# RWKV-6 attention into a tanh-shrink MLP: the first block prepared half by half, and raw weights loaded as pairs of w_in or of w_out tiles

## The chip, the cores and the metric

The kernel runs on one core of a Trainium2 chip. The metric is device time of one execution in microseconds (us). The core has four computing engines that work side by side, each through its own queue in order: PE (TensorE, matrix products into PSUM), DVE (VectorE), ACT (ScalarE) and POOL (GpSimd). SP (SyncE) does no arithmetic here; it issues DMA transfers, in order as well. Data lie in SBUF (128 partitions), results of PE in PSUM (8 banks of 512 float32 a partition).

## What is computed

```python
# attention: batch 4, heads 8, sequence 768, head size 48
for t in range(S):
    cur = einsum('bhd,bhe->bhde', u * k[t], v[t])
    y[:, :, t] = einsum('bhd,bhde->bhe', r[t], state + cur)
    state = w[t][..., None] * state + einsum('bhd,bhe->bhde', k[t], v[t])
# MLP on the 3072 tokens, model size 384, hidden size 2048
x = y.transpose(0, 2, 1, 3).reshape(B * S, H * D)
h = x @ w_in
out = (h - tanh(h)) @ w_out
```

w, the decay, lies between 0.8 and 0.95. Everything is float32.

## The kernel before, in words

**Tiling.** The 3072 tokens are cut into eight blocks of 384 (`Block(b, q)`: four batch rows, two halves of the sequence). A block's attention is done in six chunks of 64 tokens, for four pairs of heads; heads go in *halves* of two pairs each, first pairs 2 and 3, then 0 and 1 (`HALVES = (UP, 0)`). The block's MLP runs over 16 tiles (f) of 128 hidden units. While a block's MLP runs, the attention of the next block is prepared in between, from a plan written by hand (`plan(i)`), so that PE never lacks work. The first block has nobody to prepare it: a function `boot` does so before the MLP starts.

**Attention of a half.** `behind` (L403) scans w backwards inside each chunk: the product of all decays behind a token. `take_whole` (L423) picks out each chunk's whole decay. `before` (L391, L392) scans forwards. `times_behind` (L417) multiplies k by the first scan, `times_before` (L410) r by the second, and `times_u` (L428, ACT) scales k by u in place. `turn` (L487, L489) transposes the decayed k on PE and copies it out as `ks`. `own` and `earlier` are small products on PE (L463) that give the scores of a token with itself and with earlier tokens of its chunk; a predicated copy on DVE with a mask (L470) puts each into `scores`. `update_1` (L537) forms k times v for each chunk on PE, and `update_2` (L549) carries the states from chunk to chunk on DVE. `from_states` (L603) and `from_scores` (L620) add both parts of the result up in PSUM. `result_out` (L654) copies it into `xT`, and `fill_holes` (L661) moves the fourth pair, `late`, into the free rows of the three xT tiles by six small DMAs. `bound` (L434) and `held` (L439) gather what a check at the end needs.

**MLP of a tile.** `first` (L767) multiplies w_in by xT into PSUM (`hp`), ACT copies it out as h (L770), DVE squares it (L796), ACT forms qa (L799), DVE does two products (L773), and PE multiplies by w_out into three accumulators (`acc`, L844), which in block 0 follows three tiles behind `first`. Later blocks form 15 products of sums in place of 18 (`Fewer`, L891).

**Weights.** They come as 64-bit numbers in 16 units of 768 KB; unit f holds w_in and w_out of tile f (`load_weights`, L246). `convert` turns one unit into float32 by three ACT instructions (L260) and one DVE instruction (L264). Five raw buffers exist; a load into one waits until the buffer's last unit is converted. `more_weights` issues the next load on SP, and `begin_behind` makes a load wait for a named instruction.

**Order.** PE, SP, DVE and ACT run in the order in which the code issues (`manual_schedule`). In `boot`, SP issues w, k and r of the first half, the same of the second half, v and three raw units; further raw units follow behind conversions. PE starts with 97 tiny products of the identity (`passed`, L293) and later fills waits with wide ones whose result nobody reads (`busy`, L285). The second half's `behind` to `earlier` follow the first's, then one `update_1` and one `update_2` for all four pairs, `from_states` for all pairs, and `from_scores` half by half. Three units and one piece of a fourth are converted by the time tile 0 starts; then one unit a tile. `boot` has a PSUM pool of its own with four tiles of two banks, closed before the main part's pools open (one bank for hp, three for acc, two tiles of two banks for the attention). DVE clears the whole of `scores` and parts of both `states` at the start.

Of the kernel before, what the change touches and what calls it, by code (L numbers as in the profile page):

```python
# [74 lines left out]
LAST = 5  # L75
LATE = 3
# [46 lines left out]
def kernel(  # L123
# [50 lines left out]
    nc.gpsimd.memset(mask_all[0:L], 1.0)  # L174
# [5 lines left out]
    for m, at in mask_cols.items():  # L180
        if isinstance(m, str):
            masks[m] = mask_all[:, at]
            half = masks[m][0:L]
            keep(half, -1 if m == "above" else 0, [[1, L]], -1)
            if m == "diagonal":
                keep(half, 0, [[-1, L]], 1)
                continue
        else:
            width, step = (2, 1) if m == 1 else (m, 0)
            nb = L // (2 * m)  # L190
            masks[m] = mask_all[:, at].rearrange("s (b j) -> s b j", j=width)
            half = masks[m][0:L]
            keep(half, 0, [[-2 * m, nb], [0, width]], 1)
            keep(half, m - 1, [[2 * m, nb], [step, width]], -1)
        if m == "above":
            nc.gpsimd.tensor_copy(out=mask_all[L:P, 0:128], in_=mask_all[0:L, 0:128])
    nc.gpsimd.tensor_copy(out=mask_all[L:P, 128:], in_=mask_all[0:L, 128:])

    A = const.tile([P, 2, NPAIR, NCP, L], F32, name="scores", tag="scores")
    nc.vector.memset(A, 0.0)  # L200

    states = []
    for q in range(NQ):
        st = const.tile([P, NPAIR, NCH, L], F32, name=f"states{q}", tag=f"states{q}")
        nc.vector.memset(st[:, :, :, D:], 0.0)
        states.append(st)
    nc.vector.memset(states[0][:, :, 0, :], 0.0)

    w_sb = const.tile([P, NF, 2 * DM], F32, name="w_sb", tag="w_sb")
    w_in_sb = w_sb[:, :, 0:DM].rearrange("p f (i c) -> p f i c", i=KC)  # L210
    w_out_sb = w_sb[:, :, DM:2 * DM]
# [30 lines left out]
    nc.vector.memset(ones, 1.0)  # L242

    def load_weights(f, queue):
        raw = conv.tile([P, 2 * DM, 2], I32, name="raw", tag="raw")
        ins = queue.dma_start(out=raw, in_=weights[f].bitcast(I32).rearrange("p (n two) -> p n two", two=2))  # L246
        return f, raw, ins

    def convert(f, raw, _):
# [4 lines left out]
        a = w_sb[:, f, :].bitcast(I32)  # L254
# [22 lines left out]

    def scratch(ps):
        return ps.tile([P, 2, BANK], F32, name="att", tag="att")

    def busy(to, n):

        by = ident.bitcast(BF16)
# [3 lines left out]

    def passed(to, n):


        by = ident.bitcast(BF16)[:, 0:16]
        for _ in range(n):
            nc.tensor.matmul(to[0:16, 0:16], lhsT=by, rhs=by, start=True, stop=True, skip_group_check=True)  # L293
# [3 lines left out]
    class Block:  # L297
# [97 lines left out]
        def behind(self, p0, n):  # L395
            a, width = p0 * NCH * LP, n * NCH * LP
            t = self.half("post", p0, width + 1)
            nc.gpsimd.memset(t[:, width:], 1.0)
# [49 lines left out]
        def gram(self, ps, lhs, rhs, p0, n, m=None):  # L448
            width = L // 2 if m else L
            ps_t = scratch(ps)  # L450
            used = ps_t[:, :, 0:n * NCP * width]
            gr = used.rearrange("s h (p c t) -> s h p c t", p=n, c=NCP)
            for p in range(p0, p0 + n):
                for c in range(NCP):
                    for h in range(2):
                        for par in range(2):
# [6 lines left out]
                            nc.tensor.matmul(dst, lhsT=self.chunk(lhs, p, 2 * c + par)[rows], rhs=src,  # L463
                                             start=True, stop=True)
            return used

        def masked(self, ps, lhs, rhs, mask, p0):
            gr = self.gram(ps, lhs, rhs, p0, UP)
            mask = mask.bitcast(U8).unsqueeze(1).unsqueeze(1)
            return lambda: nc.vector.copy_predicated(  # L470
# [4 lines left out]
        def own(self, ps, p0):  # L475
            return self.masked(ps, "k", "r", masks["diagonal"], p0)
# [533 lines left out]
    def boot(ps, blk, later):  # L1010
        h1, h2 = HALVES
        for p0 in HALVES:
            for name in ("w", "k", "r"):
                blk.load(name, p0, UP)
# [290 lines left out]
```

## Time and profile before

| what | value |
|---|---|
| median of three runs | 558.15 us (556.01 to 560.48) |
| the profiled execution's own time | 556.46 us |
| its span, first to last instruction | 554.7 us |
| mean granted clock of PE | 0.997 |
| HBM read, written | 44.73 MB, 4.72 MB |
| shares of the chain that ended last | PE 94%, ACT 2%, DVE 2% |
| tile 0's first product starts at | 29.47 us |

The span is shorter than the execution by 1.76 us, which lie around it. In rows of the timeline the columns are start and duration in us, engine, line, operation, written tile, read tiles, shape and count; in brackets stands how long the engine had nothing to do before, and what ended that. A row of a fp32 product counts two passes, so 48 in a row are 24 products in the code. The ends of PE's rows are modelled. The main part's PE rows are almost without holes from 38.6 us on, so most of what can be seen of a change to the boot lies in the first 40 us.

### The profile page before, as it was taken

How to read it: one execution, taken by the hardware profiler on the slowest of the kernel's cores; microseconds unless marked ns; L12 is line 12 of the kernel's file. 1: busy time of each engine (PE TensorE's matmuls, PEld its weight loads, DVE VectorE, ACT ScalarE, POOL GpSimd, SP SyncE). 2: the span in 40 equal slices, each digit the busy share in tenths (PEclk: the TensorE clock that was granted, in tenths of full speed). 3: DMA queues.
4: the chain of work that ended last, by engine and by line, in shares of the span. 5: the costliest groups of instructions: out<-in, count | busy, mean ns of one | idle time of the engine just before them, and what ended most of it. 6: DMA issues, size and time to landing. Idle time of an engine off the chain costs nothing.

```text
span 554.7 us, 14151 instructions
## 1 busy us (share of the span) xinstructions
PE 537.9 (97%) x5726; PEld 404.7 (73%) x5726; DVE 463.3 (84%) x947; ACT 402.2 (73%) x811; POOL 12.0 (2%) x40
## 2 busy tenths in 40 slices
PE   4899999999999999999999999999999999999996
PEld 4646566578787787777778787777877777787774
DVE  8789999989989989878997989969897897557563
ACT  3889896697766886688866886688865986666561
POOL 6100000000000000000000000000000000000000
PEclk9999999999999999999999999999999999999999
DMA  8598473244302432236311531136122320100101
GB/s 304 207 320 301 165 215 107 72 122 115 116 13 85 100 118 74 62 94 134 109 54 44 144 116 62 52 89 157 58 88 67 80 65 4 54 1 0 44 2 46
DMA packets 53030, 56.31 MB, mean 102 GB/s; under 512 B 21472, under 2 KB 50912, under 8 KB 52960
## 3 DMA queue, kind: packets, MB, share of 16 engines
q1 hardware_dynamic: 52576, 55.18, 33.6%
q8 instruction: 46, 0.75, 0.5%
q14 instruction: 24, 0.20, 0.1%
q10 hardware_dynamic: 288, 0.10, 0.1%
q0 software_dynamic: 96, 0.07, 0.1%
HBM read 44.73 MB, written 4.72 MB: 89 GB/s over the span
## 4 chain that ended last, share of the span: by engine, by line
PE 94%; ACT 2%; DVE 2%; issue 1%; DMA 1%; SPq 0%; DVEq 0%; ACTq 0%
PE hp L767 44%; PE acc L891 26%; PE att L891 6%; PE acc L844 6%; PE att L463 2%; PE att L603 2%; PE att L620 2%; PE acc L869 2%; PE att L537 2%; DMA r<-in_rT 1%; ACT up L260 1%; PE att L487 1%; DVE scores L470 0%; PE att L285 0%; DVE pre L392 0%
## 5 line engine op out<-in xcount | busy, mean ns | idle before, releaser
L767 PE MATMUL hp<-xT,w_sb 128*128 128x384 f32 x768 | 270.1, 488 | 1.3 <-ACT h L770 1.1
L767 PEld LDWEIGHTS hp<-xT,w_sb 128*128 128x128 f32 x768 | 137.3, 190 | 75.9 <-ACT h L770 3.3
L770 ACT ACTIVATE h<-hp 128x384 f32<-128x384 f32 x128 | 62.7, 490 | 104.8 <-PE hp L767 104.7
L891 PE MATMUL acc<-forms,g 128*128 128x128 f32 x954 | 133.7, 276 | 0.5
L891 PEld LDWEIGHTS acc<-forms,g 128*128 128x128 f32 x954 | 121.6, 192 | 10.3 <-issue 1.3
L773 DVE SCALAR_TENSOR_TENSOR h<-h,s 128x384 f32<-128x384 f32 x128 | 70.7, 552 | 53.9 <-ACT s L788 53.8
L814 DVE TENSOR_TENSOR g<-g 128x256 f32<-128x256 f32 x265 | 103.3, 419 | 7.8 <-PE acc L891 7.0
L789 ACT ACTIVATE qa<-s,shift 128x384 f32<-128x384 f32 x113 | 69.6, 616 | 3.7
L791 ACT ACTIVATE junk<-s,shift 128x384 bf16<-128x384 f32 x113 | 67.7, 600 | 0.0
L773 DVE SCALAR_TENSOR_TENSOR g<-qa,h 128x384 f32<-128x384 f32 x112 | 61.7, 551 | 1.8 <-ACT qa L799 0.2
L788 ACT ACTIVATE s<-h 128x384 f32<-128x384 f32 x113 | 59.1, 523 | 3.6
L891 PEld LDWEIGHTS acc<-w_sb,g 128*128 128x128 f32 x318 | 46.7, 191 | 9.7 <-ACT sums L859 0.3
L891 PE MATMUL acc<-w_sb,g 128*128 128x128 f32 x318 | 53.1, 276 | 0.1
L891 PE MATMUL att<-w_sb,g 128*128 128x128 f32 x212 | 35.5, 275 | 0.0
L891 PEld LDWEIGHTS att<-w_sb,g 128*128 128x128 f32 x212 | 31.1, 192 | 5.3
L926 DVE TENSOR_TENSOR sums<-sums 128x256 f32<-128x256 f32 x84 | 32.9, 408 | 1.6 <-ACT sums L903 1.3
L844 PE MATMUL acc<-w_sb,sums 128*128 128x384 f32 x96 | 33.9, 489 | 0.1
L260 ACT ACTIVATE up<-raw 128x768 f16<-128x768 f32 (+1 forms) x32 | 32.0, 1070 | 0.0
L392 DVE TENSOR_TENSOR_SCAN pre<-w,start 128x780 f32<-128x780 f32 x16 | 28.5, 1783 | 0.5
L403 DVE TENSOR_TENSOR_SCAN post<-w,seed 128x780 f32<-128x780 f32 x16 | 28.5, 1783 | 0.2 <-DMA w<-in_wT 0.2
L844 PEld LDWEIGHTS acc<-w_sb,sums 128*128 128x128 f32 x96 | 17.9, 190 | 12.0 <-issue 0.2
L791 ACT ACTIVATION_READ_ACCUMULATOR junk<-s,shift 128x1 f32 x113 | 21.1, 187 | 0.0
(93 smaller groups left out, 506.5 us busy)
## 6 DMA issues: line engine op xcount, KB each, us to landing
raw<-in_weights SPq DMA_DIRECT2D x16, 768.0 KB, 5.8
w<-in_wT SPq DMA_DIRECT2D x7, 780.0 KB, 4.6
k<-in_kT SPq DMA_DIRECT2D x7, 768.0 KB, 4.5
r<-in_rT SPq DMA_DIRECT2D x7, 768.0 KB, 4.5
v_sb<-in_v SPq DMA_DIRECT2D x8, 576.0 KB, 3.9
k<-in_tokens SPq DMA_DIRECT2D x7, 576.0 KB, 3.9
r<-in_tokens SPq DMA_DIRECT2D x7, 576.0 KB, 4.9
out_y<-sums SPq DMA_DIRECT2D x18, 128.0 KB, 1.8
```

The costliest lines, as they stand in the source:

```text
L260: return lambda: nc.scalar.activation(out=to, in_=of, func=AF.Copy, scale=scale, bias=bias)
L392: return nc.vector.tensor_tensor_scan(out=self.tile("pre")[:, cols], data0=self.tile("w")[:, cols], data1=start[:, 0:n * NCH * LP], initia ...
L767: nc.tensor.matmul(hp, lhsT=w_in_sb[:, f, kc, :], rhs=xT[kc], start=(kc == KC - 1), stop=(kc == 0))
L770: return h, nc.scalar.activation(out=h, in_=hp, func=AF.Copy, scale=1.0 / UPSCALE)
L773: return lambda: nc.vector.scalar_tensor_tensor(out=out, in0=in0, scalar=scalar, in1=in1, op0=op0, op1=ALU.mult)
L788: nc.scalar.activation(out=s, in_=h, func=AF.Square)
L789: nc.scalar.activation(out=qa, in_=s, func=AF.Square, bias=shift[:, 4:5])
L791: nc.scalar.activation(out=junk[:, 0:NB], in_=s, func=AF.Relu, bias=shift[:, 5:6], accum_out=excess[:, at:at + 1])
L814: return lambda: nc.vector.tensor_tensor(out=G[:, to:to + 2], in0=two(G, g_at(q, a0), g_at(q, a1)), in1=two(G, g_at(q, b0), g_at(q, b1)), ...
L844: nc.tensor.matmul(acc, lhsT=g[:, j * P:(j + 1) * P], rhs=w_out_sb[:, f, :], start=(f == self.first), stop=(f == NF - 1))
L891: nc.tensor.matmul(to, lhsT=G[:, g_at(q, a), :], rhs=rhs, start=start, stop=stop, skip_group_check=True)
L926: ops.append(lambda op=op, at=at: nc.vector.tensor_tensor(out=at[0], in0=at[1], in1=at[2], op=OPS[op]))
```

## The change

**Loads.** Block 0's w is loaded into the tile that later holds states 0 (`states0`) and not into the tile `w`, so block 1's w has no old contents to wait for. SP issues: w of pair 3, w of pair 2, k and r of the first half, w of the second half, one raw unit, k of the second half, v, r of the second half. Three raw units, block 1's w and k and so on follow in the order of the code below, each behind the instruction named in `begin_behind`.

**Raw units.** A unit now holds w_in of two tiles or w_out of two tiles (`UNITS`), still 768 KB. The order is w_in of tiles 0 and 1, w_in of 2 and 3, w_out of 0 and 1, w_in of 4 and 5, w_out of 2 and 3, and so on. `boot` converts three units. After that `converting` issues ACT's part in pieces, a third of a unit each, by the list `PIECES` (2, 1, 2, then 3 a tile up to tile 9, then 4 a tile up to tile 12, and one piece more inside tile 1); the DVE instruction follows a tile later, ahead of the tile's other DVE work.

**Boot by halves.** The first half is taken to its end, states and result included, before the second half's result. `update_half` forms k times v for one half with the chunks side by side, `totals_by_column` (ACT) writes the chunk decays in the same layout, and `states_half` carries the states by one scan of 288 columns a pair and one small add. `from_states` reads these `first_states`. The first half's result has all its parts done before `result_out` of pairs 3 and 2; the second half's predicated copy is cut in two, so that pair 1 and pair 0 can follow one another.

**PSUM.** The main part's pools are opened before the boot, with the four banks of hp and acc as one tile. The boot takes turns among two pairs of these banks and the two attention tiles. Tiles 0, 1 and 2 write hp into three different banks.

**Memsets.** `scores` is cleared by ACT from `start`; the memsets of `states` are gone or moved (POOL, tile 14); `ones` goes to POOL; four of the masks are drawn only in the branch that is not taken here.

**Fillers.** The 97 tiny products go, as do the wide fillers before tiles 1, 2 and 3. The first `own` has 8 wide fillers ahead and 7 more that read a copy of the identity which ACT makes behind the first half's totals (`later_ident`); 2 stand ahead of the second `earlier` and 4 ahead of its `from_states`. `bound` of block 0 moves from the boot to tiles 13 and 14.

```diff
+PIECES = 2, 1, 2, 3, 3, 3, 3, 3, 3, 3, 4, 4, 4
+UNITS = [(0, 0), (0, 1)] + [u for j in range(NF // 2 - 2) for u in ((1, j), (0, j + 2))] + [(1, NF // 2 - 2),
+                                                                                      (1, NF // 2 - 1)]
...
-    nc.vector.memset(A, 0.0)
+    nc.scalar.copy(out=A.rearrange("s h p c t -> s (h p c t)").rearrange("s (n t) -> s n t", t=BANK),
+                   in_=start[:, 0:BANK].unsqueeze(1).to_broadcast([P, 2 * NPAIR * NCP * L // BANK, BANK]))
...
+        def update_half(self, ps, p0):
+            self.by_column = scratch(ps)[:, :, 0:D * NCH].rearrange("d p (e c) -> d p e c", c=NCH)
+            for x in range(UP):
+                if x:
+                    nc.tensor.drain().then_inc(fence, 1)
+                    fences.append(None)
+                    nc.tensor.wait_ge(fence, len(fences))
...
+        def totals_by_column(self, p0):
+            of = self.whole(p0, UP).rearrange("d (p c) -> d p c", c=NCH)[:, :, 1:]
+            nc.scalar.copy(out=first_totals[:, p0:p0 + UP, :, 1:],
+                           in_=of.unsqueeze(2).to_broadcast([P, UP, D, NCH - 1]))
+
+        def states_half(self, p0):
+            for p in range(UP):
+                to, by, kv = (t.rearrange("d e c -> d (e c)") for t in
+                              (first_states[:, p0 + p], first_totals[:, p0 + p], self.by_column[:, p]))
+                nc.vector.tensor_tensor_scan(out=to, data0=kv, data1=by, initial=0.0, op0=ALU.add, op1=ALU.mult)
+            return lambda kv=self.by_column: nc.vector.tensor_tensor(
+                out=states[1][:, p0:p0 + UP, 0, 0:D], in0=first_states[:, p0:p0 + UP, :, NCH - 1],
+                in1=kv[:, :, :, 0], op=ALU.add)
...
     def boot(ps, blk, later):
         h1, h2 = HALVES
+        blk.tiles["w"] = states0
+        for name, p0, n in (("w", h1 + 1, 1), ("w", h1, 1), ("k", h1, UP), ("r", h1, UP), ("w", h2, UP)):
+            blk.load(name, p0, n)
+        more_weights(nc.sync)
+        blk.load("k", h2, UP)
         blk.load_v()
+        blk.load("r", h2, UP)
...
+        blk.behind(h1 + 1, 1)
+        blk.behind(h1, 1)
         blk.take_whole(h1, UP)
+        blk.totals_by_column(h1)
+        nc.scalar.copy(out=later_ident, in_=ident)
         blk.before(h1, UP)
         blk.times_behind(h1, UP)
         blk.times_u(h1, UP)
-        blk.turn(ps, h1, ahead=97)
-        own = blk.own(ps, h1)
+        own = blk.own(ps, h1, ahead=8, late=7)
+        blk.turn_1(ps, h1)
         blk.times_before(h1, UP)
         earlier = blk.earlier(ps, h1)
-        blk.bound(h1)
-        blk.bound(h2)
+        begin_behind(blk.done, more_weights(nc.sync))
         blk.behind(h2, UP)
         blk.take_whole(h2, UP)
+        first_a, first_b = convert(*raws.pop(0))
+        run(first_a[:1])
+        blk.turn_2(h1)
+        run(first_a[1:2])
+        blk.update_half(ps, h1)
         own()
         blk.times_behind(h2, UP)
         blk.times_u(h2, UP)
-        blk.turn(ps, h2)
-        own = blk.own(ps, h2)
+        blk.turn_1(ps, h2)
+        blk.turn_2(h2)
         earlier()
+        run(first_a[2:])
+        blk.totals_by_column(h2)
+        blk.results(ps, halved=True)
+        blk.result("from_scores", both[0])
+        blk.states_half(h1)()
+        blk.result("from_states", both[0], True)
+        begin_behind(blk.opened, more_weights(nc.sync))
         blk.before(h2, UP)
+        own = blk.own(ps, h2)
+        blk.update_half(ps, h2)
         blk.times_before(h2, UP)
-        blk.update_1(ps)
...
+        earlier = blk.earlier(ps, h2, ahead=2)
+        blk.result_out((3,), nc.scalar.copy)
+        blk.result_out((2,))
+        blk.fill_holes([nc.sync, nc.gpsimd])
+        begin_behind(blk.done, later.load("w"))
+        more_weights(nc.sync)
         second_a, second_b = convert(*raws.pop(0))
         third_a, third_b = convert(*raws.pop(0))
+        run(second_a)
+        own()
+        onwards = blk.states_half(h2)
+        blk.results(ps, halved=True)
+        busy(blk.yp[0][:, 0], 4)
+        blk.result("from_states", both[1])
+        earlier(1, 1)
+        earlier(0, 1)
+        begin_behind(third_a[0](), more_weights(nc.sync))
+        run(third_a[1:2])
+        later.load("k")
         more_weights(nc.sync)
...
+        for p in reversed(both[1]):
+            blk.result("from_scores", (p,), True, more=True)
+        onwards()
         run(first_b)
         blk.result_out((1,), nc.scalar.copy)
         blk.result_out((0,), nc.vector.tensor_copy)
         run(third_a[2:])
         run(second_b)
         run(third_b)
         blk.held(0, NPAIR)
...
-            if i == 0 and f in (1, 2, 3):
-                busy(acc[0], 2)
-            h, made = first(here, f, ps_d)
+            h, made = first(here, f, banks[:, 0 if i else {1: 1, 2: 2}.get(f, 0), 0:NB])
...
+            extra = converting(pieces, PIECES[f] if f < len(PIECES) else 0) if not i else []
...
+            if i == 0 and f in (NF - 3, NF - 2):
+                blk.bound(HALVES[f - NF + 3])
+            if i == 0 and f == NF - 2:
+                nc.gpsimd.memset(states[0][:, :, 0, 0:D], 0.0)
```

More of the change, by code (lines that the diff above doesn't have):

```diff
@@ L1051, in boot @@
-        more_weights(nc.sync)
-        own()
-        blk.results(ps)
-        blk.result("from_scores", both[0])
-        run(blk.update_2())
-        run(second_a)
-        blk.result("from_states", ALL, cs=(0, 1), more=True)
-        earlier = blk.earlier(ps, h2)
-        run(third_a[:2])
-        blk.result("from_states", ALL, cs=(2,))
-        earlier()
-        idle = scratch(ps)[:, 0]
-        busy(idle, 2)
-        blk.result_out((3,), nc.scalar.copy)
-        blk.fill_holes([nc.sync, nc.gpsimd])
@@ L1116 @@
             xT = later.begin()
[L1117 removed]
+        phases, before, ahead, loads, formed_w = plan(i)
         row0 = blk.b * S + blk.q * NB
```

252 lines of the change are left out of this document (132 added, 120 removed).

## The prediction

> **What bounds the kernel now.** I read first the page's part 1 and the span, then the table of windows, then the chain of work that ended last, then each engine's timeline over the first 50 us, then the DMA issues one by one.
>
> ```profile
> span 554.7 us, 14151 instructions
> PE 537.9 (97%) x5726; PEld 404.7 (73%) x5726; DVE 463.3 (84%) x947; ACT 402.2 (73%) x811; POOL 12.0 (2%) x40
> ```
> ```profile
> 22.00:23.50 1.50, 0.22 (x14) 0.08 (x6) 0.95 (x3) 1.50 (x3) 0.00 (x0) 1.00 1.01 410
> 25.50:28.00 2.50, 2.35 (x50) 1.64 (x51) 0.82 (x2) 2.41 (x4) 1.38 (x3) 0.50 0.21 57
> 29.50:38.60 9.10, 7.88 (x25) 3.74 (x25) 6.88 (x13) 6.87 (x11) 0.00 (x0) 1.00 1.03 399
> 38.60:60.00 21.40, 21.40 (x150) 13.43 (x151) 20.58 (x37) 20.67 (x30) 0.00 (x0) 1.00 0.79 260
> 60.00:100.00 40.00, 39.90 (x396) 24.32 (x395) 38.00 (x69) 30.73 (x52) 0.13 (x2) 1.00 0.51 158
> ```
> The window rows read: stretch, length, then busy time of PE, PEld, DVE, ACT, POOL, the granted clock, DMA share, GB/s. From 38.6 on PE is busy 21.40 of 21.40 us, then 39.90 of 40.00. So the span is the moment at which PE becomes saturated plus a fixed rest, and whatever the boot saves arrives at the end one for one, as long as no later wait takes it. The change works almost wholly before that moment. I therefore price one thing: how much earlier PE reaches tile 4's first product, which started at 42.54.
>
> ```profile
> 29.47 2.17 PE L767 MATMUL hp<-xT,w_sb 128*128 128x384 f32 x6
> 42.54 2.10 PE L767 MATMUL hp<-xT,w_sb 128*128 128x384 f32 x6
> ```
> What holds the boot is VectorE. Its timeline (start, duration):
>
> ```profile
> 4.31 1.78 DVE L403 TENSOR_TENSOR_SCAN post<-w,seed 128x780 f32<-128x780 f32 x1 [0.17 <-DMA w<-in_wT]
> 6.67 1.78 DVE L392 TENSOR_TENSOR_SCAN pre<-w,start 128x780 f32<-128x780 f32 x1
> 8.37 0.93 DVE L417 TENSOR_TENSOR post<-k,post 128x768 f32<-128x768 f32 x1
> 9.22 0.96 DVE L410 TENSOR_TENSOR pre<-r,pre 128x768 f32<-128x768 f32 x1
> 10.11 1.89 DVE L403 TENSOR_TENSOR_SCAN post<-w,seed 128x780 f32<-128x780 f32 x1
> 12.53 1.03 DVE L470 COPY_PREDICATED scores<-mask_all,att 128x768 f32<-128x768 uint8 x1 [0.33 <-PE att L463]
> 13.45 0.94 DVE L417 TENSOR_TENSOR post<-k,post 128x768 f32<-128x768 f32 x1
> 19.08 0.36 DVE L549 TENSOR_TENSOR states<-att,whole 128x192 f32<-128x192 f32 x1
> 22.66 0.35 DVE L549 TENSOR_TENSOR states<-states,att 128x192 f32<-128x192 f32 x1
> 24.05 1.01 DVE L470 COPY_PREDICATED scores<-mask_all,att 128x768 f32<-128x768 uint8 x1 [1.03 <-PE att L463]
> 24.96 0.94 DVE L264 SCALAR_TENSOR_TENSOR w_sb<-w_sb,up 128x768 int32<-128x768 int32 x1
> 27.57 1.12 DVE L654 COPY xT<-att 48x384 f32<-48x384 f32 x2 [1.68 <-ACT up L260]
> ```
> It starts when the first w has landed and runs nearly without a hole to 23.0; ten state updates stand from 19.08 to 23.0 (first and last shown), then come two waits, 1.03 for scores and 1.68 for ScalarE. ScalarE is the second chain:
>
> ```profile
> 19.38 0.90 ACT L260 ACTIVATE w_sb<-raw 128x768 f32<-128x768 f32 x1
> 20.18 2.00 ACT L260 ACTIVATE up<-raw 128x768 f16<-128x768 f32 x2
> 22.01 0.90 ACT L260 ACTIVATE w_sb<-raw 128x768 f32<-128x768 f32 x1
> 24.52 0.97 ACT L654 COPY late<-att 48x384 f32<-48x384 f32 x2 [0.66 <-PE att L603]
> 31.73 0.49 ACT L770 ACTIVATE h<-hp 128x384 f32<-128x384 f32 x1 [2.24 <-PE hp L767]
> 33.95 0.59 ACT L799 ACTIVATE qa<-s,shift 128x384 f32<-128x384 f32 x1
> 89.11 0.48 ACT L654 COPY late<-att 128x384 f32<-128x384 f32 x1 [2.37 <-PE att L620]
> ```
> One raw unit costs it 22.01 - 19.38 = 2.63.
>
> **The change, step by step.** I use start-to-start steps of the rows (they are a little shorter than durations), and take the edits in the order of the path.
>
> *Start.* The first w comes as two loads of one pair each. SP issued w, k, r of the first half, the same of the second, and v 0.51 apart from 0.93 to 4.00, then the first raw unit 0.7 later; the second fence gives KB and us from issue to landing of one issue each (the r is the second half's; the last raw is the one issued at 28.1 behind block 1's w).
>
> ```profile
> 0.93 0.47 SPq L346 DMA_DIRECT2D w<-in_wT  x1
> 4.00 0.67 SPq L381 DMA_DIRECT2D v_sb<-in_v  x1
> ```
> ```profile
> w<-in_wT SPq DMA_DIRECT2D x1, 390.0 KB, 3.4
> u_sb<-in_uT ACTq DMA_DIRECT2D x1, 2.0 KB, 2.3
> r<-in_rT SPq DMA_DIRECT2D x1, 384.0 KB, 7.8
> v_sb<-in_v SPq DMA_DIRECT2D x1, 576.0 KB, 8.9
> raw<-in_weights SPq DMA_DIRECT2D x1, 768.0 KB, 10.1
> raw<-in_weights SPq DMA_DIRECT2D x1, 768.0 KB, 5.9
> ```
> 390 KB landed at 4.3, 2316 KB in all at 11.3, 2892 at 12.9, 3660 at 14.8. A load of 195 KB lies between the smallest load (0.93 + 2.3 = 3.2) and 4.3: I take 3.75, nearer the middle because the bytes halve. Two scans of 390 columns then end near 5.5 instead of 6.1. The memsets taken off VectorE are free in themselves (it waited 0.17 for w), but they would stand in the way at 3.75. Their replacement on ScalarE (1536 zeros, two small copies) fills time in which it had nothing to do until k's product at 8.4. The first mask copy of scores needs those zeros only at 11.6. POOL's shorter mask list delays nobody.
>
> *To the first half's scores.* Totals, reciprocal and scan to 7.7 (the scan started 0.58 behind the end of the first, by the rows at 4.31 and 6.67), products to 9.5, the second half's scan to 11.4, predicated copy 11.6, k's product 12.6, second predicated copy 13.4 to 14.3. The first raw unit now stands ahead of the second half's k (2700 KB in all, 12.4), v (3276 KB, 13.85) and r (14.8). k arrives just in time; v does not: the first half's update of 48 products with a drain in it (1.2, an estimate from the 1.29 for 80 below plus a drain) ends at 15.1, and VectorE idles 0.8. That is the price of the reordering.
>
> *From 15.15 on VectorE is full to tile 0.* Ten state updates (3.9 with the steps) are replaced by four scans of 288 columns, 1.78 x 288/780 = 0.65 each, and two small adds of 0.3: 3.2. To that the second half's scan with its reciprocal 2.0 (1.78 and 0.2), product 0.87, own scores 0.92, its later scores in two pieces 0.92, one conversion 0.88, and xT 1.12: 9.9 in all. So it ends at 25.05, against 28.7 before. The bounds of the new scans: 0.4 if short scans cost no more than the 0.36 row, 1.0 if PSUM input slows them; that is -1 to +1.4 over the four.
>
> *ScalarE in the same stretch.* The first half's two new scans end at 16.5 and its state products (40 at 16 ns) at 17.4; ScalarE itself, behind the second half's turned keys at 16.5, does a third piece (1.0) and totals (0.6) until 18.1; then the late copies 1.0, xT 0.5, the second unit 2.63, two pieces of the third 1.7, which is 24.0, and xT 1.0: 25.0. The two chains meet. Tile 0 thus starts its last third at 25.1 and ends at 26.6, against 29.47 + 2.17 = 31.6: 5.0 gained. The moved bounds (w's excess) leave the boot and go to tiles 13 and 14, under the 2.37 that ScalarE waits there.
>
> *PE inside it.* My steps assume a full clock:
>
> ```profile
> 9.36 1.54 PE L487 MATMUL att<-ident,post 128*128 128x128 f32 x6 [4.71 <-DVE post L417]
> 17.26 2.21 PE L537 MATMUL att<-v_sb,ks 64*64 64x48 f32 x96
> 48.34 1.47 PE L487 MATMUL att<-ident,post 128*128 128x128 f32 x12
> 53.62 1.29 PE L537 MATMUL att<-v_sb,ks 64*48 64x48 f32 x80
> ```
> Six transposes took 1.54 in the boot and twelve took 1.47 later: the boot's PE ran at half rate until 19, though the clock column reads 1.00 there. The 15 wide fillers put ahead of the first scores (8 from 2.1, 7 once ScalarE has copied their operand at about 6.5) run almost up to 9.4. After the first half's later scores, at 12.0, PE has nothing until v lands. The Trainium skill, "TensorE: Matmul & The Clock Gate", Part 1, says that the gate opens after about 3.4 us of busy array and shuts after an idle window of that length. The rows at 9.36 and 48.34 agree with the first; by the rule the new fillers open the gate, and a hole may shut it.
>
> *From tile 0 to tile 4.* Three PSUM banks let tiles 0 to 2 follow each other; PE then waits for ScalarE. h of tile 0 at 26.7; the fourth unit should start at 27.05 but its load stands on SP behind three small loads and block 1's w, which wait for xT and the second half's scores (20.7): issue 22.3 plus the 5.9 that such a unit took behind w, 28.2. I put the loss at 0.9. Then ScalarE and VectorE take turns (2.63 and the rows at 31.73 and 33.95, some 3.6 a tile, beside block 1's scans on VectorE), and h of tile 3 comes at 37.3, so tile 4 starts at about 37.9 to 38.3 instead of 42.54: 4.2 to 4.6 gained. After that ScalarE owes one unit more than before (three pieces), paid by four pieces a tile in tiles 10 to 12, where it had waits for PE; I count nothing. The fetch stall of 22.0 to 23.5, when PE was busy 0.22, is taken as not coming back, since PE's boot has far fewer instructions.
>
> *Sum.* A gain of 4.2: the profiled execution took 556.46 (1.8 above its span), so 552.3 by its own time. The median of the runs shown, 558.15, is 1.7 higher: 554.0.
>
> **The rivals.**
> *The clock is lost* (most of the boot at half rate). For it: the window 25.5 to 28.0 shows 0.50 after the thin stretch 22.0 to 23.5, and the new boot has PE idle from 12 to 13.9; against it: the dense work from 14 on and 15 wide fillers. Half rate from 13 to 19 makes some 136 products of the first half's chain (16 ns each by the 53.62 row, 1.29/80) up to 16 ns longer, 2.2, and the transposes beside VectorE 0.8: I take 1.9. With the second half's products, too, 3.5. The gain is then 2.3 or 0.7: 556 to 557.5. By the skill's rule it would be the first of these only.
> *More than forecast.* If w lands at 3.4, v 0.5 sooner, the scans take 0.4 and the fourth unit is in time, these give 0.3 + 0.5 + 1.0 + 0.9 on top: up to 6.9, 551.3. Nothing speaks against any one, and the scans with one other suffice for 1%; all four together are unlikely.
> *Slower: weights late behind SP's order.* Units used to be asked for early (five by 20); now the fourth waits for the second half's last score product. Each us that this comes later moves ScalarE's whole row by one. The gain is gone if that unit lands at 32.5, so if SP passes at 26.6 and not 22.3. Beyond it, every later unit queues behind w and k at the DMA rate of the 29.5 to 38.6 row (share 1.03, full), and a loss of 6 is reached at 38.5: 564. Against it: at that point SP stands behind nothing but PE's work priced above.
> *Nothing changes*, since both chains of the boot are replaced by equally long ones: I see no stage for it, its time is that of the lost clock.
>
> **How the numbers follow.** A measurement tells about 1% (5.6 us) from no change. Forecast (gain 2.5 to 5.6): 0.40. Lost clock (-1 to 2.5): 0.12. More than forecast (over 5.6): 0.36, since most unknown costs lie on that side of my choices. Late weights: 0.12. So faster by over 1% 0.36, within 0.52, slower 0.12. Likeliest 554.0, its own range 552.5 to 555.7; the range for 8 in 10 reaches from the best case with runs as low as the lowest shown (547.5) to the lost clock with the highest (560).
>
> **What would show it.** Right: the first scan at or before 3.9; transposes near 110 ns apart from 10 on; the first half's states near 15.2; tile 0's first product ending near 26.6 and tile 4's start near 38; PE full from there. Wrong: PE's boot products at their old pace, h waiting for conversions that wait for raw loads beyond 29, a new hole in PE in tiles 9 to 13, or a clock below 1.00 after 26.

## The result, and the profile after

The changed kernel took 2745.07 us (median of 6 runs, 2742.43 to 2748.44) against 558.22 (6 runs, 555.64 to 560.48) for the kernel before on the same chip: a ratio of 4.92, 95% interval 4.904 to 4.936. The forecast of 554.0 and its range were far off.

The page of the changed kernel shows at once that more work was done: 2.4 times the instructions, PE busy for 59% of the span and not 97%, and a granted clock (the row PEclk, in tenths of full speed, 40 slices of 68.6 us) that falls after slice 9. PEld is PE's loading of weights.

```profile
span 2745.7 us, 34046 instructions
...
PE 1611.3 (59%) x14125; PEld 1023.5 (37%) x14125; DVE 1021.1 (37%) x2159; ACT 897.0 (33%) x1815; POOL 8.1 (0%) x43
...
PE   7889988985554455445545553555455545554554
...
PEclk9999999997677567757775776577667756775777
```

The windows table (same columns as in the prediction) splits the span into the pass, which now has holes, and what comes behind it.

```profile
60.00:100.00 40.00, 36.41 (x381) 21.05 (x380) 34.74 (x63) 33.00 (x53) 0.13 (x2) 1.00 0.43 145
100.00:540.00 440.00, 393.05 (x3971) 283.64 (x3969) 329.90 (x668) 280.85 (x589) 0.92 (x11) 1.00 0.28 74
540.00:640.00 100.00, 87.28 (x621) 61.63 (x622) 50.49 (x127) 50.89 (x116) 0.44 (x2) 1.00 0.05 14
640.00:2740.00 2100.00, 1046.91 (x8491) 629.42 (x8490) 557.97 (x1222) 488.73 (x998) 2.33 (x9) 0.70 0.07 21
```
The kernel before had PE busy 39.90 of 40.00 from 60 to 100, and 439.36 of 440 from 100 to 540. Here PE has holes in the whole pass, which therefore ends near 645. After 640 come 2100 us more, with 8491 rows of PE.

*The 2100 us.* The end of the program tests conditions on the hidden values and on w, which it has counted on the way (`again`, L1307). If one does not hold, a general version of the whole computation is run (`If(anew > 0)`). The timeline at 638 shows the test, and then that this branch, which the section on the change calls not taken, is entered: POOL draws the four masks for it, VectorE clears the states, SP loads v afresh.

```profile
638.63 0.14 DVE L1307 TENSOR_SCALAR again<-att 1x1 int32<-1x1 f32 x1 [0.30 <-PE att L1304]
639.49 0.23 POOL L187 MEMSET mask_all<- 64x160 int8 x1 [180.79 <-DVE again L1307]
...
644.93 0.79 DVE L1325 MEMSET states<- 128x384 f32 x2
...
645.21 0.39 SPq L392 DMA_DIRECT2D v_sb<-in_v  x1
```

*Why the condition fails.* Look for the copies that take the first half's result out of PSUM. The late copies (pair 3) start at 18.37. The copy of pair 2 is next on ScalarE, and its result was finished with pair 3's, yet it stands 3.06 and is released by a product of L478, which is the second half's later scores:

```profile
18.37 0.97 ACT L712 COPY late<-att 48x384 f32<-48x384 f32 x2 [0.66 <-PE att L660]
...
21.42 0.93 PE L478 MATMUL acc<-pre,post 48*64 48x64 f32 x48
...
22.41 0.48 ACT L712 COPY xT<-acc 128x384 f32<-128x384 f32 x1 [3.06 <-PE acc L478]
...
22.93 0.76 DVE L614 TENSOR_TENSOR_SCAN first_states<-acc,first_totals 128x288 f32<-128x288 f32 x1 [2.21 <-ACT xT L712]
```
A copy of a result has no business waiting for scores. `Turns` hands out four two-bank pieces in a ring and asks nobody whether the piece is free. In `boot`, `earlier` of the second half (L1129) stands in the code ahead of `result_out` of pairs 3 and 2, and it gets the two banks in which pair 2's result still lies. In the order of the program the scores come first, so the program lets the copy wait for them, and xT of pair 2 receives scores. VectorE's first scan of the second half, which reads another part of the same tile of four banks, waits behind it (2.21).

*The holes in the first pass.* The waits, grouped (engine, line, what ended the wait; us in total, times, longest):

```profile
PEld acc L948 <- ACT h L827: 77.7, 65, 1.2
...
PE acc L948 <- ACT h L827: 37.8, 65, 0.6
...
PE acc L824 <- ACT sums L960: 11.2, 12, 1.2
...
PE acc L901 <- ACT h L827: 7.5, 12, 1.1
```
L948 and L901 accumulate into acc, L827 is ScalarE's copy of h out of hp. They share no number, only the PSUM tile. One tile of the pass on the timeline:

```profile
589.10 2.10 PE L824 MATMUL acc<-xT,w_sb 128*128 128x384 f32 x6
591.24 0.49 ACT L827 ACTIVATE h<-acc 128x384 f32<-128x384 f32 x1 [1.82 <-PE acc L824]
591.79 1.16 PE L948 MATMUL acc<-forms,g 128*128 128x128 f32 x8 [0.58 <-ACT h L827]
```
PE ends the products of hp at 591.20, stands 0.58 while ScalarE copies, and only then goes on with products into other banks.

### The profile page after: what moved, and what is told of

The parts are those of the page before. It is cut to its first block, busy times and chain, and to the rows that moved or that the text cites. A ratio compares the mean times of both kernels' runs of the same rounds, so it can differ in the third digit from the quotient of the medians.

```text
span 2745.7 us, 34046 instructions
## 1 busy us (share of the span) xinstructions
PE 1611.3 (59%) x14125; PEld 1023.5 (37%) x14125; DVE 1021.1 (37%) x2159; ACT 897.0 (33%) x1815; POOL 8.1 (0%) x43
## 4 chain that ended last, share of the span: by engine, by line
PE 55%; DVE 17%; ACT 16%; DMA 4%; issue 4%; SPq 2%; PEld 1%; PEldq 0%; DVEq 0%; ACTq 0%
PE acc L901 20%; PE hp L824 11%; PE acc L824 9%; DVE h L830 5%; PE att L478 5%; PE acc L948 5%; ACT h L827 4%; DVE sums L887 3%; DVE sums L830 3%; DVE th L883 3%; ACT qa L879 3%; ACT s L878 2%; ACT qb L880 2%; ACT th L881 2%; DVE post L771 2%
## 5 line engine op out<-in xcount | busy, mean ns | idle before, releaser
L901 PE MATMUL acc<-w_sb,sums 128*128 128x384 f32 x864 | 542.7, 794 | 754.8 <-DVE sums L887 745.4
L901 PEld LDWEIGHTS acc<-w_sb,sums 128*128 128x128 f32 x864 | 250.8, 310 | 1009.2 <-DVE sums L887 827.8
L883 DVE TENSOR_TENSOR th<-h,th 128x384 f32<-128x384 f32 x128 | 71.5, 558 | 1196.8 <-ACT th L881 1196.8
L827 ACT ACTIVATE h<-hp 128x384 f32<-128x384 f32 x128 | 63.0, 492 | 1113.6 <-PE hp L824 1113.6
L824 PE MATMUL acc<-xT,w_sb 128*128 128x384 f32 x768 | 273.0, 492 | 17.6 <-ACT sums L960 12.4
L478 PE MATMUL att<-pre,post 48*64 48x32 f32 (+1 forms) x4560 | 132.8, 281 | 146.2 <-DVE pre L771 105.0
L830 DVE SCALAR_TENSOR_TENSOR h<-h,s 128x384 f32<-128x384 f32 x256 | 142.5, 557 | 136.7 <-ACT s L845 131.4
L478 PEld LDWEIGHTS att<-pre,post 48*64 48x64 f32 x4560 | 123.2, 206 | 159.5 <-issue 154.6
L824 PEld LDWEIGHTS acc<-xT,w_sb 128*128 128x128 f32 x768 | 137.6, 191 | 95.9 <-ACT sums L960 14.8
L948 PE MATMUL acc<-forms,g 128*128 128x128 f32 x954 | 137.3, 280 | 19.8 <-ACT h L827 18.6
L948 PEld LDWEIGHTS acc<-forms,g 128*128 128x128 f32 x954 | 119.0, 192 | 40.9 <-ACT h L827 38.3
L827 ACT ACTIVATE h<-acc 128x384 f32<-128x384 f32 x128 | 62.9, 492 | 187.2 <-PE acc L824 187.1
L887 DVE COPY_PREDICATED sums<-big,th 128x384 f32<-128x384 int32 x128 | 75.0, 586 | 13.6 <-DVE sums L830 0.5
L478 PE MATMUL att<-r,k 48*64 48x64 f32 x816 | 26.8, 309 | 90.5 <-ACT r L805 87.5
L880 ACT ACTIVATE qb<-s,shift 128x384 f32<-128x384 f32 x128 | 77.1, 603 | 0.0
```

Source lines behind the costliest of these rows:

```text
L478: self.done = nc.tensor.matmul(dst, lhsT=self.chunk(lhs, p, 2 * c + par)[rows], rhs=src, start=True, stop=True)
L824: nc.tensor.matmul(hp, lhsT=w_in_sb[:, f, kc, :], rhs=xT[kc], start=(kc == KC - 1), stop=(kc == 0))
L827: return h, nc.scalar.activation(out=h, in_=hp, func=AF.Copy, scale=1.0 / UPSCALE)
L830: return lambda: nc.vector.scalar_tensor_tensor(out=out, in0=in0, scalar=scalar, in1=in1, op0=op0, op1=ALU.mult)
L880: nc.scalar.activation(out=qb, in_=s, func=AF.Square, bias=shift[:, 1:2])
L883: nc.vector.tensor_tensor(out=th, in0=h, in1=th, op=ALU.subtract)
```

## The experiments

The first five kernels settle the two large faults, the other seven what was left of the forecast. All ratios are to the kernel before, run on the same chip.

**e1: the branch is never taken.**

```diff
-    nc.vector.tensor_single_scalar(again, sure[0:1, 0, 0:1], float(P * (n_whole + n_excess + n_top)),
-                                   op=ALU.not_equal)
+    nc.vector.tensor_single_scalar(again, sure[0:1, 0, 0:1], -1.0,
+                                   op=ALU.is_lt)
```


> The changed kernel, but the branch at the end never goes back to the general path (its output is then whatever the first pass left; the repeat of all blocks is left out). Theory: the trace of the changed kernel shows the first pass ending near 645 us and the general path filling 2100 us behind it, so this run takes about 647 us. Rival: the first pass is as quick as forecast and the trace's 645 holds work of the general path already; then 550 to 560.

Measured: 651.98 us in one run, close to the theory. This kernel leaves out the repeat, so its output is not the result that is wanted. The branch is 2093 of the 2187 us lost. What remains is the first pass with its holes.

**e2: copies ahead of the reuse.**

```diff
-        earlier = blk.earlier(ps, h2, ahead=2)
         blk.result_out((3,), nc.scalar.copy)
         blk.result_out((2,))
+        earlier = blk.earlier(ps, h2, ahead=2)
```


> The changed kernel with one thing moved: pairs 3 and 2 of the first half are copied out before the second half's later scores take the same two PSUM banks. Theory (the copy of pair 2 reads banks that those scores have overwritten, and the kernel's own test of the hidden values therefore sends it into the general path): the general path is not entered, 640 to 648 us. Rival (the test is tripped by something else that moved, such as the bound on w, now read in tiles 13 and 14 from a tile that is then cleared): nothing changes, 2745 us.

Measured: 649.36 us (2 runs, 648.88 to 649.84; ratio 1.166, 1.161 to 1.171), just above the theory's range. Three lines in another order keep the program out of the branch, and w's bound, which this kernel tests as the changed one does, was not the cause. PE was busy 392.95 of the 440 us from 100 to 540, as in the changed kernel.

**e3: besides that, banks apart.** The boot's two pairs are in a pool of their own, closed behind the boot; hp and the three acc are tiles of one bank each. Tiles 0 to 2 keep three banks.

```diff
-    banks = ps_d.tile([P, 4, BANK], F32, name="acc", tag="acc")
-    boot(Turns([banks[:, 0:2], banks[:, 2:4]] + ps_a.both), blocks[0], blocks[1])
-    acc = [banks[:, j] for j in range(1, 4)]
+    with tc.tile_pool(name="ps_boot", bufs=1, space=PSUM) as ps_boot:
+        pairs = [ps_boot.tile([P, 2, BANK], F32, name=f"pair{j}", tag=f"pair{j}") for j in range(2)]
+        boot(Turns(pairs + ps_a.both), blocks[0], blocks[1])
+    ps_d = mains.enter_context(tc.tile_pool(name="ps_d", bufs=1, space=PSUM))
+    hp = ps_d.tile([P, BANK], F32, name="hp", tag="hp")
+    acc = [ps_d.tile([P, BANK], F32, name=f"acc{j}", tag=f"acc{j}") for j in range(NB // P)]
...
-            h, made = first(here, f, banks[:, 0 if i else {1: 1, 2: 2}.get(f, 0), 0:NB])
+            h, made = first(here, f, (hp if i else {1: acc[0], 2: acc[1]}.get(f, hp))[:, 0:NB])
```


> As the run before, and hp and the three accumulators are four tiles of one bank each again, in a pool opened behind the boot's, which is closed. Theory (with all four banks in one tile every product on an accumulator waits for ScalarE's copy of hp, and the reverse, about 0.6 to 0.75 us a tile of the MLP over some 120 tiles): the first pass loses its 85 us and the boot shows what was forecast for it, 550 to 556 us. Rival (the first pass is slow because the raw weights come late and ScalarE falls behind): still over 600 us.

Measured: 553.74 us (9 runs, 552.37 to 556.96; ratio 0.9945, 0.9922 to 0.9968). The pass has no holes left:

```profile
100.00:540.00 440.00, 439.38 (x4540) 340.82 (x4540) 368.96 (x775) 321.85 (x684) 0.66 (x10) 1.00 0.28 75
```
And with a tile to each bank, a product runs while ScalarE reads the bank beside it:

```profile
32.52 4.03 PE L824 MATMUL acc<-xT,w_sb 128*128 128x384 f32 x12
...
32.77 0.49 ACT L827 ACTIVATE h<-hp 128x384 f32<-128x384 f32 x1 [0.61 <-PE hp L824]
```
The Trainium skill, "PSUM — Partial Sum Buffer", section "PSUM bank collisions raise a hardware error", says that two engines must not be on one bank and quadrant at once, and that the same pairs on different banks run clean. These two rows agree with the second half of that; no run here shows the first. So the wait for h in the changed kernel was not asked for by the banks: the program put it there because the banks were one tile.

**e4: the kernel before with hp and acc in one tile, and nothing else.**

```diff
-    acc = [ps_d.tile([P, BANK], F32, name=f"acc{j}", tag=f"acc{j}") for j in range(NB // P)]
+    banks = ps_d.tile([P, 4, BANK], F32, name="acc", tag="acc")
+    acc = [banks[:, j] for j in range(1, 4)]
...
-            h, made = first(here, f, ps_d)
+            h, made = first(here, f, banks[:, 0, 0:NB])
```


> The kernel before with only this changed: hp and the three accumulators become one PSUM tile of four banks. Theory (the shared tile alone costs the waits): 635 to 650 us, that is 80 to 90 more than before. Rival (the cost comes from the boot or the weights): within 5 us of the kernel before.

Measured: 651.64 us (2 runs; ratio 1.170, 1.165 to 1.176), just above the theory's range, with the same row in the waits (L890 and L769 are L948 and L827 of the changed kernel):

```profile
PEld acc L890 <- ACT h L769: 78.2, 65, 1.7
```
The shared tile alone costs some 95 us, with none of the new boot.

**g4: banks apart, but the copies still behind the reuse** (e3 without e2's move).

> The changed kernel (2745 us) with the boot's pairs in a pool of their own and hp and the sums in tiles of one bank each, but the results of the first half still copied after their pair of banks is handed out again. Theory (two causes that do not touch each other): the general path is entered after the first pass, which ends at about 553, so 2745 less the 92 to 96 of the shared tile, 2640 to 2660. Rival (the shared tile is what sends it to the general path): about 554.

Measured: 2645.64 us in one run, inside the theory's range. That completes the square: both faults 2745, only the order wrong 2646, only the tile shared 649, neither 554. They add to within 4 us, and neither causes the other.

**g2: only the sums share a tile, hp has its own** (based on f4, below).

```diff
-    acc = [ps_d.tile([P, BANK], F32, name=f"acc{j}", tag=f"acc{j}") for j in range(NB // P)]
+    banks = ps_d.tile([P, 3, BANK], F32, name="acc", tag="acc")
+    acc = [banks[:, j] for j in range(3)]
```


> Copies ahead of the reuse, pairs apart, hp in one bank of its own (552.5 us), but the three banks of sums as one tile. Theory (sharing a tile costs where one engine writes one bank while another reads the other; the sums are read only at the end of each block's pass, hp in every tile): less than 2 per block end, 552.5 to 558, and no waits on copies of h in the middle of a pass. Rival (any products into banks of one tile wait for each other's readers at every tile): waits like those of the changed kernel, 580 or more.

Measured: 564.08 us (4 runs; ratio 1.016, 1.011 to 1.020): neither value. The place is the theory's, since no wait for h is left in the pass and the new waits stand where the sums are read, at the ends of blocks. The size, put at under 6 in all, is some 12 against f4. Part of it is not the waits themselves: behind the longest of PE's, 2.11 us ahead of 105.86, the clock is at 0.50 from 108 to 110.

```profile
PEld acc L948 <- ACT sums L960: 5.2, 7, 1.0
PEld acc L901 <- ACT o L916: 3.9, 2, 2.7
```

**f4: e3 with hp in one bank for all tiles.**

```diff
-            h, made = first(here, f, (hp if i else {1: acc[0], 2: acc[1]}.get(f, hp))[:, 0:NB])
+            h, made = first(here, f, hp[:, 0:NB])
```

> The same kernel (553.7 us) with hp of tiles 0, 1 and 2 in one bank, as in the kernel before, and not in three. Theory of the prediction (three banks let tiles 0 to 2 follow each other): each of tiles 1 and 2 waits for ScalarE's copy of the h ahead, 0.5 and more each, and tile 4 starts 0.5 to 1.5 later: 554.3 to 555.5. Rival (ScalarE and VectorE set the pace from tile 0 to tile 4, so PE only waits earlier): tile 4 starts where it did, 553.3 to 554.1.

Measured: 552.51 us (10 runs, 552.07 to 557.21; ratio 0.9928, 0.9896 to 0.9961), the fastest of all here and faster than theory and rival said, though its interval overlaps e3's. Tile 4 starts at 38.99. In f1, which keeps the three banks and had a hole in the boot of like size (1.12 against 0.86), it starts at 38.42, but at half rate:

```profile
34.91 1.56 PE L901 MATMUL acc<-w_sb,sums 128*128 128x384 f32 x4 [0.78 <-ACT h L827]
38.42 3.76 PE L824 MATMUL hp<-xT,w_sb 128*128 128x384 f32 x6 [1.95 <-ACT h L827]
```
```profile
38.99 2.10 PE L824 MATMUL hp<-xT,w_sb 128*128 128x384 f32 x6
```
With three banks, tiles 0 to 2 are done sooner and PE then stands longer in one piece. The windows of f1 show the granted clock following:

```profile
35.00:38.40 3.40, 1.47 (x4) 0.58 (x4) 3.26 (x8) 2.75 (x5) 0.00 (x0) 1.00 1.01 397
...
40.00:41.60 1.60, 1.60 (x4) 0.94 (x3) 1.60 (x5) 1.50 (x3) 0.00 (x0) 0.50 0.96 357
```
In f1, PE was busy 1.47 of the 3.40 us ahead of tile 4, with no idle piece over 1.95, and the clock fell to 0.50. The Trainium skill, "TensorE: Matmul & The Clock Gate", Part 1, puts the fall behind at least one idle window of about 3.4 us; here less idle time was enough. But it did not have to fall: e3 has the same stretch ahead of its tile 4, and f3 one like it (busy 1.46, idle piece 1.96), and both kept the full clock. For e3:

```profile
39.55:42.95 3.40, 1.47 (x4) 0.59 (x4) 3.26 (x8) 2.76 (x5) 0.00 (x0) 1.00 0.98 366
42.95:44.55 1.60, 1.58 (x5) 1.05 (x6) 1.50 (x3) 1.60 (x3) 0.00 (x0) 1.00 0.79 190
```
So one profile can't tell what the banks do. The clocks of all executions say more, in the two pairs of kernels that differ in the banks alone: the mean granted clock was 0.998 or more in 3 of e3's 9 executions and 8 of f4's 10, and in 1 of f1's 10 and 6 of the 12 of g1 (f4 with f1's early load). In these executions e3 took 552.4 to 552.8, f4 552.1 to 553.0, f1 552.1 and g1 552.7 to 553.1. The rival was thus right in its core: ScalarE and VectorE set the pace. With the clock kept, three banks gain nothing that can be seen here, though tile 4 starts 0.57 sooner in f1; with one bank the clock was kept more often. Where the executions without a profile lost it is not known.

**f1 and f2: the hole in PE's boot.** In e3's profiled execution (556.96, the slowest of its nine) PE stands 3.49 at a place where nothing that the profile shows releases it (`issue` in the row). The kernel before had 1.28 at such a place. f1 asks for the third raw unit sooner, f2 later. Both start from e3 and take out `begin_behind(blk.opened, more_weights(nc.sync))`. f1:

```diff
         begin_behind(blk.done, more_weights(nc.sync))
+        more_weights(nc.sync)
         blk.behind(h2, UP)
```
f2:

```diff
-        begin_behind(blk.done, later.load("w"))
+        begin_behind(blk.done, more_weights(nc.sync))
+        later.load("w")
         more_weights(nc.sync)
```

> The kernel is the one with copies ahead of the reuse and the boot's pairs apart (553.7 us), with one edit: the third raw unit is asked for right behind the second (about 12.8) and not when the first state product has run (about 17.1). In the profiled run of the unedited kernel PE stood 3.49 us (19.54 to 23.02) for its instructions; the one packet of the instruction queue in that stretch moved between 20 and 21, while the bytes of the third unit (asked for at 17.1) were still moving (DMA share 0.95 from 18 to 20). Theory (the packet of instructions queues behind the bytes of the raw unit): all of it has landed by about 18.5, the packet moves by 19.5, the hole is at most 1.3 as in the kernel before, tile 0 starts by 28 and the time is 551 to 552.5. Rival (the hole belongs to that place of PE's program, whatever the transfers do): a hole of 2 to 3.5 at the same product, 553 to 554.5.

> The same kernel (553.7 us), but the third raw unit is asked for behind the small loads of xT (about 19.5 to 22) and not at 17.1. Theory (instructions queue behind raw bytes): nothing moves when the instructions are asked for, the hole in PE shrinks to 1.3 or less; but ScalarE needs the third unit at about 22 and gets it at 26 or later, which costs at most what ScalarE had to spare there (6.33 us of waiting in the profiled run with the hole, about 2.5 without it): 552.5 to 555. Rival (the place in the program): the hole stays at 2 to 3.5, and the late unit adds nothing, because ScalarE waits out the hole anyway: 553.5 to 555, told apart by the hole and not by the time.

Measured: f1 553.89 us (10 runs; ratio 0.9950, 0.9925 to 0.9975), f2 556.24 us (10 runs; ratio 0.9992, 0.9971 to 1.0012). The holes of both are the theory's, 1.12 each; f1's time is the rival's. The rows at the end of the hole in e3, f2 and f4, one fence each, each with the idle time in the bracket:

```profile
23.02 0.46 PE L599 MATMUL pair<-v_sb,ks 64*64 64x48 f32 x8 [3.49 <-issue]
```
```profile
20.47 0.33 PE L599 MATMUL pair<-v_sb,ks 64*64 64x48 f32 x8 [1.12 <-issue]
```
```profile
20.25 0.33 PE L599 MATMUL pair<-v_sb,ks 64*64 64x48 f32 x8 [0.86 <-issue]
```
The window from 19 to 20, just ahead of the hole's end, for f2 and then f4 (last three columns: clock, DMA share, GB/s):

```profile
19.00:20.00 1.00, 0.34 (x16) 0.22 (x16) 1.00 (x2) 1.00 (x3) 1.00 (x3) 1.00 0.10 22
```
```profile
19.00:20.00 1.00, 0.39 (x16) 0.26 (x16) 1.00 (x2) 1.00 (x2) 1.00 (x3) 1.00 0.90 362
```
f2 has hardly a transfer in flight and a hole of 1.12; f4, which asks for the third unit where e3 does, has the DMA engines nearly full and 0.86. So a hole of about 1 stands without raw bytes. The DMA views, read in steps of 0.1 us, show more: one packet of the instruction queue moves ahead of each hole, and the hole ends 2.2 to 2.6 us behind it, whatever its length. The packet moved at 17.7 in f4, 17.9 in f1, 18.0 in f2, 18.5 in g1 (its hole is 2.12 and ends at 21.05) and 20.7 in e3. In f1 it moved among raw bytes (DMA share 0.81 from 17 to 18), and the hole was no longer than f2's: raw bytes alone do not make the hole long. f4 is no test of that, since its packet had moved before its raw bytes (share 0.06 from 17 to 18). Why the packet came about 3 us later in e3 than in f4 stays open.

f2's time missed both ranges: ScalarE waited 4.56 for the late unit, and tile 4 started at 41.95.

**f3: e3 without the wide fillers ahead of the first scores.**

```diff
-        nc.scalar.copy(out=later_ident, in_=ident)
...
-        own = blk.own(ps, h1, ahead=8, late=7)
+        own = blk.own(ps, h1)
```

> The same kernel (553.7 us) without the 15 wide fillers ahead of the first scores and the copy of their operand. Theory (they set the clock of the boot): the first six transposes take 1.54 as in the kernel before and not 0.87, the products of the boot run at half rate until about 19, and VectorE waits for PE 1 to 2 us more before its last xT copy: 554.5 to 556. Rival (VectorE is the bound of the boot and hides PE's rate): the transposes are as slow, but the late copies still start at 18.0 to 18.4 and the time is 553 to 554.5. Second effect: PE's program is 15 products shorter ahead of the hole, so that a hole for instructions comes 15 products later in the boot, or goes.

Measured: 555.20 us (10 runs; ratio 0.9975, 0.9952 to 0.9998), inside the theory's range, though the interval overlaps e3's. The profile decides: six transposes take 1.54 again (0.87 in e3), the late copies start at 19.97 and not 17.99. PE has no hole at L599 here: its 48 rows stand in one piece from 20.41, so in a program that is 15 products shorter PE does not stand at that place.

```profile
10.93 1.54 PE L500 MATMUL pair<-ident,post 128*128 128x128 f32 x6
...
19.97 0.97 ACT L712 COPY late<-att 48x384 f32<-48x384 f32 x2 [0.68 <-PE att L660]
```

**g1: f4 with f1's early third unit.**

> Copies ahead of the reuse, pairs apart, hp in one bank (552.5 us), and the third raw unit asked for right behind the second. Theory (two things are still lost in some executions: a long hole for PE's instructions while a raw unit moves, and half a clock at tile 4 when three banks let tiles 0 to 2 run ahead and PE then stands 1.95): both are gone, tile 4's six products take 2.2 in the profile, the median is 552.0 to 552.6. Rival (the early unit costs the second half's r or the small loads of xT as much as it saves): 552.8 to 554.

Measured: 553.72 us (12 runs; ratio 0.9943, 0.9917 to 0.9970): the rival's range, and no better than f4 or e3. In its profile tile 4's six products take 2.10, as the theory said, but the boot has a hole of 2.12, and the clock is at 0.50 behind it, from 22 to 24.

**g3: f4 with the first raw unit behind the second half's k, v and r.**

```diff
-        more_weights(nc.sync)
         blk.load("k", h2, UP)
         blk.load_v()
         blk.load("r", h2, UP)
+        more_weights(nc.sync)
```

> Copies ahead of the reuse, pairs apart, hp in one bank (552.5 us), with the first raw unit asked for behind the second half's k, v and r, as in the kernel before, and not ahead of them. Theory (the prediction's price of 0.8 for v's late landing): PE's hole of 1.24 to 1.35 ahead of the first half's state update goes, VectorE's totals start 0.8 sooner, tile 0 starts 0.5 to 0.8 sooner: 551.7 to 552.1. Rival (ScalarE pays for it, whose first unit then lands at about 13 and not at 10.7, and its late copies start later): 552.5 to 554.

Measured: 556.79 us (12 runs; ratio 1.0003, 0.9985 to 1.0021): the rival, and larger than it said. ScalarE runs in order, and the first conversion stands ahead of its copy of the turned keys (ks):

```profile
14.66 0.89 ACT L263 ACTIVATE w_sb<-raw 128x768 f32<-128x768 f32 x1 [4.77 <-DMA raw<-in_weights]
15.45 0.79 ACT L506 COPY ks<-pair 128x768 f32<-128x768 f32 x1
```
```profile
16.29 1.47 PE L599 MATMUL att<-v_sb,ks 64*64 64x48 f32 x48 [3.76 <-ACT ks L506]
```
In f4 that first conversion starts at 10.82 and PE's L599 at 13.51. Tile 4 starts at 43.14 here and at 38.99 there.

## Why the prediction was wrong

**The step that failed** is the PSUM part of "From tile 0 to tile 4": "Three PSUM banks let tiles 0 to 2 follow each other". I read the edit as more banks, and never asked what waits one tile of four banks brings, nor who may still be reading a piece that `Turns` gives out. Both were to be read in the code: L1129 stands above L1130, and hp and acc are slices of one tile. The sum has no term for either. The price of the shared tile is some 95 us (e4, and e2 against e3); of the early reuse, 2093 (e1). Even with tiles apart, three banks gain nothing that can be seen (e3 against f4). My slower rival put a loss at SP's order of weights, with 564 as its price; f2 and g3 show that this mechanism exists, but it was not what happened.

**"The span is the moment at which PE becomes saturated plus a fixed rest"** was right for every kernel without the two faults, f1 and g2 aside. Time of the profiled execution less the start of tile 4: before 556.46 - 42.54 = 513.9, e3 514.0, f2 514.2, f3 514.0, f4 513.7, g1 513.6, g3 513.7. f1 has 515.5, with the half clock that starts just at that tile, and g2, whose sums share a tile, 523.4. In the changed kernel, the rest was not fixed: that is where the shared tile acted.

**The boot's own sum** nearly comes out once the faults are gone, in part by luck. Forecast gain 4.2: f4's ratio gives 4.0 (2.2 to 5.8) of 557.08, e3's 3.1 (1.8 to 4.3) of 556.28.
- First scan: forecast 3.75. f4 has it at 3.65.
- End of tile 0's first product: forecast 26.6. Measured 27.68 in f4 and f1, 1.1 later: VectorE, which was to be full until then, waited 1.2 for PE's `from_scores` (L678); PE's hole ahead of that, which the sum left out, is of like size (0.86 and 1.12).
- Late copies: forecast 18.1. Measured 18.37 in the changed kernel and 17.84 to 17.99 in f4 and e3.
- The new scans: forecast 0.65 each. Measured 1.40 for two.
- The wait for the fourth raw unit: forecast 0.9. ScalarE waited 0.42 in f1 and 0.53 in f4, which makes up for part of the 1.1.
- Tile 4: forecast 37.9 to 38.3. Measured 38.42 (f1) and 38.99 (f4), but 40.27 in f3 and 42.97 in e3 with its long hole.
- The full clock that the steps assume was right for the transposes, thanks to the wide fillers: 0.87 against 1.54 (f3).

Two slips in the working bear on none of this. The low end of the range, 547.5, does not follow from its own words: 551.3 less the 2.1 between the median and the lowest run is 549.2. And the "last third" of tile 0's product has 1.5 us ahead of it in the sum, which is two thirds.

**Smaller steps that failed.** The fetch stall, "taken as not coming back": it came back in the same stretch, at 0.70 in the changed kernel and up to 3.49 in e3. "The price of the reordering", 0.8 of idle VectorE for v: the idle time was there (0.68 in f4), but it is no price, since the old order costs about 4 more (g3), because ScalarE's ks stands behind the first raw unit.

## What to carry to other kernels

Before pricing an edit that merges buffers, list for each of them who writes and who reads it at the same time: here one tile shared by parts with different readers made PE's writes to any part wait for ScalarE's reads of another, and that cost some twenty times what the edit was worth. Where a ring gives out pieces by count, check in program order that the last reader stands ahead of the next taker; a copy that waits for an unrelated product in the trace is the sign of it. Where a program tests its own data and may take another path, an edit's effect on those data has a price in time too.

## What the runs showed of the hardware that was not expected

- The clock fell to 0.50 after 3.40 us in which PE was still busy for 1.47 (f1), and behind idle pieces of 2.12 (g1) and 2.11 (g2). It did not fall behind the same stretch in e3 and f3, so how long PE stood does not decide it alone. In f4 the same products stand spread out, and PE was busy 2.20 and 3.39 in the two stretches at the same places as in f1, with the clock kept:

```profile
31.50:34.90 3.40, 2.20 (x6) 1.06 (x6) 2.95 (x5) 2.65 (x6) 0.00 (x0) 1.00 1.04 429
35.00:38.40 3.40, 3.39 (x11) 2.06 (x12) 3.26 (x8) 2.76 (x5) 0.00 (x0) 1.00 1.00 397
```
- PE's hole at a fixed place of its program was between 0.47 (e2) and 3.49 us (e3) with the same instructions around it, with full and with idle DMA engines, and ended 2.2 to 2.6 us after a packet of the instruction queue had moved.
